# An attention and gated MLP kernel: nine pieces of fill among each of the last three pairs' ends, their stores on ScalarE's queue, and the first pair's order k, q, rests

## The chip, the cores and the metric

The kernel runs on one core of one Trainium2 chip. A core has a matrix engine (TensorE, PE in the views; PEld is its weight load), VectorE (DVE), ScalarE (ACT), GpSimd (POOL), and SyncE (SP), which here only issues transfers. ScalarE issues transfers too, from its own queue. The metric is the time of one execution in microseconds on the device.

## The reference

A linear attention whose features are `exp(±(x @ w_phi - max|x @ w_phi|))`, and behind it an MLP with a gate, on 4608 tokens (8 batches of 576), 8 heads of 64, model width 512, inner width 1536.

```python
def phi(x):
    proj = np.einsum('bhsd,df->bhsf', x, w_phi)
    proj = proj - np.max(np.abs(proj), axis=-1, keepdims=True)
    return np.concatenate([np.exp(proj), np.exp(-proj)], axis=-1)
q_p, k_p = phi(q), phi(k)
kv = np.einsum('bhsf,bhsd->bhfd', k_p, v)
num = np.einsum('bhsf,bhfd->bhsd', q_p, kv)
x = num / (np.einsum('bhsf,bhf->bhs', q_p, k_p.sum(2))[..., None] + 1e-6)   # then to (tokens, 512)
xn = x / np.sqrt(np.mean(x * x, axis=-1, keepdims=True) + 1e-6) * rms_g
g = xn @ w_gate
out = (g / (1 + np.exp(-g)) * (xn @ w_val)) @ w_out
```

## The kernel before

Products are made to nearly float32's precision from operands that are split into a high and a low part (`_split`: a ScalarE copy to the high part, a VectorE subtraction for the low one) and three matmuls each. The instructions are written in Python order, and a scheduler that works with modelled times orders them on each engine. `late()` restrains it: what is written inside is issued only after the latest instruction so far of ScalarE, VectorE and GpSimd. A queue of transfers runs in its own order, and an issue that has to wait holds up what is behind it.

**Stage one, the attention.** The loop over `i` works on 32 pairs of heads (`PR = 32`; a batch has four pairs) as a pipeline of four parts, merged by `_merge` at chosen fractions of an iteration: `front(i)` transposes q, k and the rests (the last 64 tokens of q and k together, "r") and projects them; `mid(i-1)` takes the exponentials and sums `kv` into `acc`; `back(i-2)` computes numerators and denominators (`num`) and, in `inv`, sends the denominators through memory and back (`dd`, `dr`, a reciprocal on VectorE, `di`, `rc`) to spread their inverses; `last(i-3)` multiplies (`fin`) and stores to `xs`. The loop has three more iterations than pairs, in which the last pairs' ends run. Each iteration also decodes a piece of the MLP's weights.

**Fill.** When a batch is finished, two blocks of 288 columns of `xs` are ready for the first 3 of 12 column tiles of the MLP's two first products, without the norm, which is applied later. `load_x` fetches a block (two slots of x, on ScalarE's queue), `fill` splits it (`xo`) and gives six pieces (`unit`): 12 matmuls into `fp`, a ScalarE copy to `fo` (three buffers), and a store to `gvs`. There are 16 blocks and so 96 pieces. A quota issues some at the end of each iteration, as long as more than `RES = 30` pieces are left. What is left runs behind the loop, six at a time.

**Block 0 of stage two** is fetched at i = 27 (`x0`), into one of the two slots, so that `load_x` rests in iterations 27 and 28; `prep(0)`, its norm, is written after iteration 29.

**Stage two** runs the other 9 column tiles in 12 blocks of 384 columns (`gv`), `gv_raw` the 3 from the fill, and stage three the last product.

Of the kernel before, what the change touches and what calls it, by code (L numbers as in the profile page):

```python
# [58 lines left out]
def _split(nc, hi, lo, x, hi_copy=None, lo_eng=None):  # L59
    (hi_copy or nc.scalar.copy)(hi, x)  # L60
    (lo_eng or nc.vector).tensor_tensor(lo, x, hi.bitcast(F32), ALU.subtract)  # L61


def _merge(streams):


    todo = []
    for n, st in enumerate(streams):
        for i, piece in enumerate(st):
            at = (i + 0.5) / len(st)  # L70
            if isinstance(piece, tuple):
                at, piece = piece
            todo.append((at, n, i, piece))
    for _, _, _, piece in sorted(todo, key=lambda t: t[:3]):
        piece()


def _spread(pieces, a, b):
    return [(a + (b - a) * (n + 0.5) / len(pieces), p) for n, p in enumerate(pieces)]
# [3 lines left out]
def kernel(ctx: ExitStack, tc: tile.TileContext, q, k, v, w_phi,  # L83
                         w_gate, w_val, w_out, rms_g, out):
    nc = tc.nc
# [4 lines left out]
    N = B * S  # L90
# [6 lines left out]
    J1 = 3  # L97
    T = 384
    NB = N // T
    TF = S // 2  # L100
# [26 lines left out]
    gvv = gvs.rearrange("(j w p) n -> j p w n", w=2, p=128)  # L127
# [12 lines left out]
    def fetch(bk, n=T, queue=None):  # L140
        x = xips[-1 if bk % 2 else 0].tile([128, NC * T], F32, name="x")[:, 0:NC * n].rearrange("p (c t) -> p c t", c=NC)
        (queue or nc.sync).dma_start(out=x, in_=xsv[:, :, bk * n:(bk + 1) * n])
        return x
# [23 lines left out]
    ps_f = ctx.enter_context(tc.tile_pool(name="ps_f", bufs=2, space=PSUM))  # L167
# [3 lines left out]
    waiting = set()  # L171

    @contextmanager
    def late():

        ins = nc.cur_bb.bb.instructions
        n = len(ins)
        with ExitStack() as es:
            for eng in LATE:
                for i in reversed(ins[-300:]):  # L180
                    if i.engine == eng and i.name not in waiting:
                        es.enter_context(tc.issue_after(i))
                        break
            yield
        waiting.update(i.name for i in nc.cur_bb.bb.instructions[n:])
# [27 lines left out]

    vms = [const.tile([128, 2, T0, D + 1], F32, name=f"vm{i}") for i in range(3)]
    vrs = [const.tile([128, 2, D + 1], F32, name=f"vr{i}") for i in range(3)]
    for vm, vr in zip(vms, vrs):
        nc.gpsimd.memset(vm, 1.0)
        nc.gpsimd.memset(vr, 1.0)
        nc.gpsimd.memset(vr[64:128, 0], 0.0)
        nc.gpsimd.memset(vr[0:64, 1], 0.0)  # L220
# [31 lines left out]
    def decode_pieces(jobs, dec):  # L252
        raws = {}

        def piece(i):
            if i == 0:
                raws[0] = _fetch(nc, dec, *jobs[0][:2])
            raw = raws.pop(i)
            if i + 1 < len(jobs):
                raws[i + 1] = _fetch(nc, dec, *jobs[i + 1][:2])  # L260
            with late():
                jobs[i][2](_decode(nc, dec, raw, jobs[i][1]))
        return [lambda i=i: piece(i) for i in range(len(jobs))]
# [22 lines left out]
    def front(pr):  # L286
        d = st[pr]
        f = {n: d[n].rearrange("p h t d -> p (h t d)") for n in ("kt", "qt")}
        us = {n: [f[n + "t"][:, i * 128:(i + 1) * 128] for i in range(4)] for n in "kq"}
        us["r"] = [d["rb"].rearrange("p a d -> p (a d)")]  # L290
        d["y"] = {}
        hl = {}

        def trans(n):
            m = len(us[n]) * 128
            tp = ps_s.tile([128, 512], F32, name="sm")
            for j, u in enumerate(us[n]):
                nc.tensor.transpose(out=tp[:, j * 128:(j + 1) * 128], in_=u, identity=ident)
            th = wk.tile([128, 512], F32R, name="th")
            tl = wk.tile([128, 512], F32R, name="tl")  # L300
            _split(nc, th[:, 0:m], tl[:, 0:m], tp[:, 0:m])
            hl[n] = (th, tl)

        def proj(n, u0):
            th, tl = hl[n]
            m = min(2, len(us[n]) - u0)
            pp = ps_p.tile([128, 4, F], F32, name="pp")
            for j in range(m):
                o = pp[:, 2 * j:2 * j + 2].rearrange("p a f -> p (a f)")
                cs = slice((u0 + j) * 128, (u0 + j + 1) * 128)  # L310
                nc.tensor.matmul(o, th[:, cs], wh, start=True, stop=False)  # L311
                nc.tensor.matmul(o, th[:, cs], wl, start=False, stop=False)
                nc.tensor.matmul(o, tl[:, cs], wh, start=False, stop=True)  # L313
            mx = wk.tile([128, 4], F32, name="mx")
            nc.vector.tensor_reduce(mx[:, 0:2 * m], pp[:, 0:2 * m], axis=AX.X, op=ALU.max,  # L315
                                    apply_absolute_value=True)
            y = wk.tile([128, 4 if n != "r" else 2, F], F32, name="y" + n, bufs=3 if n != "r" else 2)
            nc.vector.tensor_tensor(y[:, 0:2 * m], pp[:, 0:2 * m],  # L318
                                    mx[:, 0:2 * m].unsqueeze(2).broadcast_to([128, 2 * m, F]), ALU.subtract)
            d["y"][n, u0 // 2] = y  # L320

        return [lambda: trans("r" if pr else "k"), lambda: trans("k" if pr else "r"),
                lambda: proj("r", 0), lambda: proj("k", 0), lambda: trans("q"), lambda: proj("k", 2), lambda: proj("q", 0), lambda: proj("q", 2)]

# [132 lines left out]
    fills = []  # L457
    blocks = list(range(N // TF))

    def fill(bk, x):  # L460
        xhl = xfp.tile([128, 2, NC, TF], F32R, name="xo")
        xx = dict(h=xhl[:, 0], l=xhl[:, 1])
        with late():
            for c in range(0, NC, 2):
                _split(nc, *(a[:, c:c + 2] for a in (xx["h"], xx["l"], x)))

        def unit(j, wi):
            js = slice(j * 128, (j + 1) * 128)
            fp = ps_f.tile([128, T], F32, name="fp")
            i = 0  # L470
            for c in range(NC):
                a, al = wf1[wi][0][:, c, js], wf1[wi][1][:, c, js]
                for w, x in ((a, "h"), (a, "l"), (al, "h")):
                    nc.tensor.matmul(fp[:, 0:TF], w, xx[x][:, c], start=(i == 0), stop=(i == 3 * NC - 1))  # L474
                    i += 1
            o = xm.tile([128, T], F32, name="fo", bufs=3)[:, 0:TF]
            nc.scalar.copy(o, fp[:, 0:TF])  # L477
            nc.sync.dma_start(out=gvv[j][:, wi, bk * TF:(bk + 1) * TF], in_=o)
        return [lambda j=j, wi=wi: unit(j, wi) for j in range(J1) for wi in range(2)]

    PR = B * NP
    early, decs_late = decode_jobs()
    decs = decode_pieces(early, dec)
    RES = 5 * J1 * 2
    units, here = [], []
    dq = quota = 0.0

    def load_x():
        while fills and len(here) < 2:
            bk = fills.pop(0)  # L490
            here.append((bk, fetch(bk, TF, nc.scalar)))

    def landed():
        if here:
            units.extend(fill(*here.pop(0)))

    load(0)
    nc.sync.dma_start(out=g, in_=rms_g.rearrange("(c p) -> p c", p=128))
    load(1)
    for i in range(PR + 3):  # L500
        streams = []
        if i < PR:
            streams.append(_spread(front(i), -0.2, 0.7))
        if 0 <= i - 1 < PR:
            streams.append(_spread(mid(i - 1), -0.2, 1.1))
        if 0 <= i - 2 < PR:
            streams.append(back(i - 2))
        if 0 <= i - 3 < PR:
            streams.append(last(i - 3))
        dq += 1  # L510
        dl, decs = decs[:int(dq)], decs[int(dq):]
        dq -= int(dq)
        streams.append(dl)
        _merge(streams)

        if i == PR - 3:
            with late():
                nxt = prep(0, x0, ps_f, "fp")
        if len(units) <= 3:
            landed()  # L520
        if len(units) + (len(fills) + len(here)) * J1 * 2 > RES:
            quota += (N // TF * J1 * 2 - RES) / (PR - 4)
            nf = int(quota)
            quota -= nf
            now, units[:] = units[:nf], units[nf:]
            _merge([now])
        if i == PR - 5:
            x0 = fetch(0)
        if not PR - 5 <= i < PR - 3:
            load_x()  # L530
        if i + 2 < PR:
            load(i + 2)
    while units or here or fills:
        if len(units) <= 6:
            landed()
        now, units[:] = units[:6], units[6:]
        _merge([now])
        load_x()
    a_ctx.close()

# [86 lines left out]
    PRE = 4  # L627
    wos_ops = []
    load_gv(0)
    xb = {0: nxt}  # L630

    LAST = [*range(JL, JN), *range(JL)]
    for bk in range(NB):
# [172 lines left out]
```

## Time and profile before

| | us |
|---|---|
| median of 3 runs | 1333.65 (1332.86 to 1335.17) |
| the profiled execution | 1339.35 |
| its span in the trace | 1337.6 |

The engines' busy time over the whole span is in the page's first section. A row of the windows gives, for a stretch of time, the busy time of each engine and the clock that TensorE was granted (1.00 is full). A row of the timeline has its start, its length, engine, line, operation, what is written from what (buffer numbers left out) and, in brackets, how long the engine stood before it and what ended that. "x12" is a group of 12.

### The profile page before, as it was taken

What the parts mean: (1) busy time and instruction counts of PE and PEld (TensorE: products, weight loads), DVE (VectorE), ACT (ScalarE), POOL (GpSimd) and SP (SyncE); (2) the same over time, 40 slices, a digit from 0 to 9 for tenths busy, and PEclk for the clock granted to TensorE, in tenths of its full rate; (3) what the DMA queues carried; (4) which work ended last, traced back from release to release, by engine and by line L of the source; (5) the groups of instructions that cost most, each with busy time, mean ns of one, the idle gap of its engine ahead of it and who ended that gap; (6) DMA issues with size and microseconds to landing.
All of it is one profiled execution on the core that took longest, in us unless ns stands there. A gap on an engine that the chain in (4) does not pass through costs nothing.

```text
span 1337.6 us, 25479 instructions
## 1 busy us (share of the span) xinstructions
PE 1288.5 (96%) x9396; PEld 1275.6 (95%) x9396; DVE 885.0 (66%) x1301; ACT 711.0 (53%) x1510; POOL 605.5 (45%) x568
## 2 busy tenths in 40 slices
PE   7989999999999896899999999999999999999998
PEld 7989899999999896899999999999999999999998
DVE  7899788778778773313456656655534498777784
ACT  5988877778778782434344344443333334434332
POOL 3766565555555570000233223233221078788684
PEclk9999999999999898999999999999999999999999
DMA  5555556566555434843454454554433534554451
GB/s 159 127 147 156 161 158 165 167 170 169 157 164 161 123 95 127 249 153 126 141 170 140 157 168 133 166 168 140 133 115 108 183 111 126 150 166 127 142 168 54
DMA packets 204524, 197.22 MB, mean 147 GB/s; under 512 B 69552, under 2 KB 186416, under 8 KB 204400
## 3 DMA queue, kind: packets, MB, share of 16 engines
q1 hardware_dynamic: 186448, 181.44, 45.2%
q10 hardware_dynamic: 17952, 14.16, 3.8%
q8 instruction: 74, 1.21, 0.4%
q14 instruction: 50, 0.41, 0.1%
HBM read 126.04 MB, written 69.50 MB: 146 GB/s over the span
## 4 chain that ended last, share of the span: by engine, by line
PE 57%; DMA 3%; DVE 1%; ACT 0%; issue 0%; POOL 0%; ACTq 0%; SPq 0%; DVEq 0%
PE fp L588 17%; PE gp L588 16%; PE gd L742 6%; PE gz L742 6%; PE gy L742 5%; PE fp L474 4%; PE fp L742 3%; DMA wc<-wvs 1%; DMA gvs<-fo 1%; DMA rc<-di 0%; PE sm L415 0%; DMA dd<-nd 0%; ACT fo L477 0%; POOL s2l L61 0%; DVE a12l L61 0%
## 5 line engine op out<-in xcount | busy, mean ns | idle before, releaser
L380 POOL TENSOR_TENSOR ql<-eq,qh 128x256 fp32r<-128x256 f32 x256 | 217.7, 882 | 67.3 <-issue 39.5
L588 PE MATMUL gp<-xb,wv 128*128 128x384 f32 x864 | 161.9, 334 | 0.8 <-ACT wv L60 0.8
L588 PE MATMUL fp<-xb,wg 128*128 128x384 f32 x864 | 161.0, 334 | 0.0
L573 DVE TENSOR_TENSOR h<-sl,gp 128x384 f32<-128x384 f32 x108 | 59.6, 552 | 144.2 <-PE gp L588 75.6
L588 PEld LDWEIGHTS gp<-xb,wv 128*128 128x128 f32 x864 | 150.7, 188 | 1.0 <-ACT wv L60 1.0
L571 ACT ACTIVATE sl<-fp 128x384 f32<-128x384 f32 x108 | 52.8, 489 | 185.6 <-PE fp L588 170.7
L588 PEld LDWEIGHTS fp<-xb,wg 128*128 128x128 f32 x864 | 150.7, 188 | 0.0
L54 POOL TENSOR_TENSOR wa<-raw,wa 128x192 f32<-128x192 f32 (+1 forms) x112 | 66.2, 613 | 162.2 <-issue 58.6
L351 PE MATMUL acc<-vm,ek 128*128 128x65 f32 x1024 | 131.8, 271 | 0.0
L315 DVE TENSOR_REDUCE mx<-pp 128x4 f32<-128x512 f32 (+1 forms) x160 | 100.6, 632 | 43.0 <-PE pp L313 41.5
L351 PEld LDWEIGHTS acc<-vm,ek 128*128 128x128 f32 x1024 | 128.1, 195 | 0.4 <-ACT ek L338 0.4
L151 POOL TENSOR_TENSOR ss<-ss,sq 128x384 f32<-128x384 f32 x36 | 37.6, 1044 | 160.6 <-ACT sq L150 160.6
L61 POOL TENSOR_TENSOR xb<-x,xb 128x1536 fp32r<-128x1536 f32 x12 | 42.5, 3540 | 132.3 <-ACT xb L60 124.6
L474 PE MATMUL fp<-xo,fg 128*128 128x288 f32 x576 | 92.8, 302 | 5.7 <-ACT fo L477 3.4
L376 ACT ACTIVATE qh<-sm 128x512 fp32r<-128x512 f32 (+1 forms) x192 | 97.3, 507 | 0.0
L474 PE MATMUL fp<-xo,fv 128*128 128x288 f32 x576 | 92.2, 300 | 4.4 <-ACT fo L477 4.4
L311 PE MATMUL pp<-wh,th 128*128 128x256 f32 x288 | 89.0, 310 | 2.7 <-DVE yr L318 2.1
L474 PEld LDWEIGHTS fp<-xo,fg 128*128 128x128 f32 x576 | 81.7, 190 | 7.4 <-ACT fo L477 4.4
L474 PEld LDWEIGHTS fp<-xo,fv 128*128 128x128 f32 x576 | 81.7, 190 | 5.1 <-ACT fo L477 5.1
L61 POOL TENSOR_TENSOR s2l<-st,s2h 128x768 fp32r<-128x768 f32 x18 | 43.5, 2419 | 95.0 <-ACT s2h L60 47.6
L375 ACT ACTIVATE eq<-sm 128x512 f32<-128x512 f32 x128 | 78.4, 612 | 14.1 <-PE sm L364 13.2
L313 PE MATMUL pp<-wh,tl 128*128 128x256 f32 x288 | 83.0, 298 | 1.8 <-DVE tl L61 1.8
(198 smaller groups left out, 3801.8 us busy)
## 6 DMA issues: line engine op xcount, KB each, us to landing
hs<-h SPq DMA_DIRECT2D x144, 192.0 KB
ht<-hs SPq DMA_DIRECT2D x18, 1536.0 KB
gvs<-fo SPq DMA_DIRECT2D x96, 144.0 KB
gvr<-gvs SPq DMA_DIRECT2D x36, 384.0 KB
rc<-di SPq DMA_DIRECT2D x32, 288.0 KB
x<-xs ACTq DMA_DIRECT2D x16, 576.0 KB
x<-xs SPq DMA_DIRECT2D x12, 768.0 KB
kt<-in_k_dram SPq DMA_DIRECT2D x32, 256.0 KB
```

What stands on the lines that cost most here:

```text
L54: nc.gpsimd.tensor_tensor(a[:, h], lf[:, h], a[:, h], ALU.mult)
L61: (lo_eng or nc.vector).tensor_tensor(lo, x, hi.bitcast(F32), ALU.subtract)
L311: nc.tensor.matmul(o, th[:, cs], wh, start=True, stop=False)
L313: nc.tensor.matmul(o, tl[:, cs], wh, start=False, stop=True)
L315: nc.vector.tensor_reduce(mx[:, 0:2 * m], pp[:, 0:2 * m], axis=AX.X, op=ALU.max, apply_absolute_value=True)
L351: nc.tensor.matmul(acc[:, sg, h], e[h][:, sg, j], vm[:, h, j], start=False, stop=(h == 1 and j == T0 - 1))
L375: nc.scalar.activation(ei[:, sg], yi, AF.Exp, scale=1.0 - 2.0 * sg)
L376: nc.scalar.activation(hi[:, sg], yi, AF.Exp, scale=1.0 - 2.0 * sg)
L380: nc.gpsimd.tensor_tensor(lo[:, sg, cs], ei[:, sg, cs], hi[:, sg, cs].bitcast(F32), ALU.subtract)
L474: nc.tensor.matmul(fp[:, 0:TF], w, xx[x][:, c], start=(i == 0), stop=(i == 3 * NC - 1))
L588: nc.tensor.matmul(gp[:, 0:T], w, e[:, c], start=(i == 0), stop=(i == 3 * NC - 1))
L742: nc.tensor.matmul(place[n], a[:, kp], w[:, o], start=(first and kp == 0 and i == 0), stop=(kp == KP - 1 and i == 2), skip_group_check=True)
```

## The change

```diff
@@ late()
-                    if i.engine == eng and i.name not in waiting:
+                    if i.engine == eng and i.name not in waiting and not isinstance(i, mybir.InstDMACopy):
@@ the constant tiles
-    for vm, vr in zip(vms, vrs):
+    for vm in vms:
         nc.gpsimd.memset(vm, 1.0)
+    for vr in vrs:
         nc.gpsimd.memset(vr, 1.0)
@@ front(pr)
+        if pr == 0:
+            return [lambda: trans("k"), lambda: proj("k", 0), lambda: trans("q"), lambda: proj("k", 2),
+                    lambda: trans("r"), lambda: proj("r", 0), lambda: proj("q", 0), lambda: proj("q", 2)]
@@ fill(bk, x)
-        def unit(j, wi):
+        def unit(j, wi, queue):
...
-            nc.sync.dma_start(out=gvv[j][:, wi, bk * TF:(bk + 1) * TF], in_=o)
-        return [lambda j=j, wi=wi: unit(j, wi) for j in range(J1) for wi in range(2)]
+            queue.dma_start(out=gvv[j][:, wi, bk * TF:(bk + 1) * TF], in_=o)
+        return [lambda q=None, j=j, wi=wi: unit(j, wi, q or nc.sync) for j in range(J1) for wi in range(2)]
...
+    END = 9
+    nxt = []
@@ load_x() and landed()
-            here.append((bk, fetch(bk, TF, nc.scalar)))
+            here.append((bk, fetch(0, T, nc.scalar) if bk is None else fetch(bk, TF, nc.scalar)))
...
-        if here:
+        if here and here[0][0] is None:
+            with late():
+                nxt.append(prep(0, here.pop(0)[1], ps_f, "fp"))
+        elif here:
             units.extend(fill(*here.pop(0)))
+
+    def more():
+        if len(units) <= 3:
+            landed()
+            load_x()
+        if units:
+            units.pop(0)(nc.scalar)
@@ the loop over i
+        if i >= PR:
+            streams.append([more] * END)
         _merge(streams)
-        if i == PR - 3:
-            with late():
-                nxt = prep(0, x0, ps_f, "fp")
...
+        if i < PR:
...
-        if i == PR - 5:
-            x0 = fetch(0)
-        if not PR - 5 <= i < PR - 3:
-            load_x()
+        if i == PR + 1:
+            fills.append(None)
+        load_x()
...
     while units or here or fills:
...
-        _merge([now])
+        _merge([[lambda u=u: u(nc.scalar) for u in now]])
```

The quota issues pieces only while `i < PR`. In the three iterations behind, nine calls of `more` are merged among the ends of the last pairs; each issues one piece, and splits and fetches a block when three or fewer are left. Their stores, and those of all pieces behind the loop, go to ScalarE's queue; the quota's stay on SP's. Block 0's fetch and norm go through the list of fills (the entry `None`), put there at i = 33, ahead of the last batch's two blocks. x is fetched in iterations 27 and 28 too. `late()` does not take a transfer for an engine's latest instruction any more. In the first pair the rests come behind k and q.

Of the fill's 1152 matmuls, 408 stood ahead of the last pair's transposes of q, 114 from there to the last numerators, and 630 behind; now it is 504, 72 and 576.

The first place is on ScalarE, at the end of the third last pair's k exponentials. There `wa` and `raw` are the decoding of a weight, `ss` and `sq` the squares of block 0's norm, `eqr` and `qh` the exponentials of the rests of q. Before:

```order
L48 ACTIVATE wa<-raw 128x384
L49 ACTIVATE raw<-raw 128x384
L147 ACTIVATE ss<-x 128x384
L150 ACTIVATE sq<-x 128x384
L375 ACTIVATE eqr<-sm 128x128
L376 ACTIVATE qh<-sm 128x2x64
```

Now:

```order
L48 ACTIVATE wa<-raw 128x384
L49 ACTIVATE raw<-raw 128x384
L379 ACTIVATE eqr<-sm 128x128
L380 ACTIVATE qh<-sm 128x2x64
L379 ACTIVATE eqr<-sm 128x128
```

The squares left this place; the norm now stands on ScalarE behind the attention, among the copies of fill.

The second place is on VectorE at the end of the attention. `yq` is the last pair's projection of q, `nd` the multiplication in `fin`, `dr` the reciprocal in `inv`, `kv1l` the low part of the last pair's `kv`, and `xo` the split of a block of fill. Before:

```order
L318 TENSOR_TENSOR yq<-pp,mx 128x512
L442 TENSOR_TENSOR nd<-nd,rc 64x576
L443 TENSOR_TENSOR nd<-nd,rc 64x576
L425 RECIPROCAL dr<-dr 128x9
L55 TENSOR_TENSOR wa<-wp,wa 128x384
L442 TENSOR_TENSOR nd<-nd,rc 64x576
L443 TENSOR_TENSOR nd<-nd,rc 64x576
L425 RECIPROCAL dr<-dr 128x9
L61 TENSOR_TENSOR kv1l<-acc,kv1h 128x4x65
L61 TENSOR_TENSOR xo<-x,xo 128x576 x2
```

Now:

```order
L319 TENSOR_TENSOR yq<-pp,mx 128x512 x2
L446 TENSOR_TENSOR nd<-nd,rc 64x576
L447 TENSOR_TENSOR nd<-nd,rc 64x576
L429 RECIPROCAL dr<-dr 128x9
L55 TENSOR_TENSOR wa<-wp,wa 128x384
L61 TENSOR_TENSOR kv1l<-acc,kv1h 128x4x65
L61 TENSOR_TENSOR xo<-x,xo 128x576 x2
L446 TENSOR_TENSOR nd<-nd,rc 64x576
L447 TENSOR_TENSOR nd<-nd,rc 64x576
L61 TENSOR_TENSOR xo<-x,xo 128x576 x2
L429 RECIPROCAL dr<-dr 128x9
```

One pair's `nd` and the next one's `dr` moved from ahead of `kv1l` to behind it.

The third place is where the last pair's result is stored (`xs`), on SP's queue, with the transfers of its denominators and the fill's stores (`gvs`). Before:

```order
L419 DMA dd<-nd 1x576
L478 DMA gvs<-fo 128x288
L423 DMA dr<-dd 128x9
L478 DMA gvs<-fo 128x288
L426 DMA di<-dr 128x9
L478 DMA gvs<-fo 128x288
L428 DMA rc<-di 64x1152
L478 DMA gvs<-fo 128x288 x2
L448 DMA xs<-nd 128x64
L449 DMA xs<-nd 128x512
L478 DMA gvs<-fo 128x288 x31
```

Now, on SP's queue:

```order
L423 DMA dd<-nd 1x576
L453 DMA xs<-nd 128x512
L427 DMA dr<-dd 128x9
L430 DMA di<-dr 128x9
L432 DMA rc<-di 64x1152
L452 DMA xs<-nd 128x64
L453 DMA xs<-nd 128x512
```

And on ScalarE, from there on (`wc` is a tile of stage two's weights, cast to `wg` and `wv`):

```order
L481 COPY fo<-fp 128x288
L579 DMA wc<-wgs 128x4x128
L482 DMA gvs<-fo 128x288
L579 DMA wc<-wvs 128x4x128
L142 DMA x<-xs 128x4x288
L481 COPY fo<-fp 128x288
L60 CAST wg_0_8791<-wc 128x512
L579 DMA wc<-wgs 128x4x128
L482 DMA gvs<-fo 128x288
```

The stores left SP's queue there and stand on ScalarE's, between its copies, the x loads and the weight loads.

More of the change, by code (lines that the diff above doesn't have):

```diff
@@ L513 @@
         streams.append(dl)
+        if i >= PR:
+            streams.append([more] * END)
         _merge(streams)
-        if i == PR - 3:
-            with late():
-                nxt = prep(0, x0, ps_f, "fp")
[L519 to L525, printed above, removed]
-            _merge([now])
-        if i == PR - 5:
-            x0 = fetch(0)
-        if not PR - 5 <= i < PR - 3:
-            load_x()
+        if i < PR:
+            if len(units) <= 3:
+                landed()
+            if len(units) + (len(fills) + len(here)) * J1 * 2 > RES:
+                quota += (N // TF * J1 * 2 - RES) / (PR - 4)
+                nf = int(quota)
+                quota -= nf
+                now, units[:] = units[:nf], units[nf:]
+                _merge([now])
+        if i == PR + 1:
+            fills.append(None)
+        load_x()
         if i + 2 < PR:
@@ L536 @@
         now, units[:] = units[:6], units[6:]
-        _merge([now])
+        _merge([[lambda u=u: u(nc.scalar) for u in now]])
         load_x()
@@ L629 @@
     load_gv(0)
-    xb = {0: nxt}
+    xb = {0: nxt[0]}
     LAST = [*range(JL, JN), *range(JL)]
```

## The prediction

> **What bounds the kernel now.** I read the page's first section, then busy time by stretch, then single stretches in order of time.
>
> ```profile
> span 1337.6 us, 25479 instructions
> PE 1288.5 (96%) x9396; PEld 1275.6 (95%) x9396; DVE 885.0 (66%) x1301; ACT 711.0 (53%) x1510; POOL 605.5 (45%) x568
> ```
>
> TensorE is busy 1288.5 of 1337.6 us. The change takes no matmul away, so it can gain only from TensorE's 49 idle us, and from time in which TensorE runs at half its clock. The windows show where that is (columns: stretch, its length, busy time of PE, PEld, DVE, ACT, POOL, then the granted clock, DMA share, GB/s).
>
> ```profile
> core 0: us, PE busy (x) PEld busy (x) DVE busy (x) ACT busy (x) POOL busy (x), PEclk, DMA share, GB/s
> 60.00:100.00 40.00, 35.50 (x289) 34.03 (x289) 37.91 (x69) 34.53 (x87) 26.48 (x34) 1.00 0.56 150
> 100.00:425.00 325.00, 319.15 (x2629) 314.49 (x2628) 263.59 (x458) 253.46 (x632) 187.05 (x229) 1.00 0.59 164
> 425.00:620.00 195.00, 174.49 (x1260) 170.62 (x1259) 87.17 (x135) 106.48 (x246) 53.33 (x61) 0.95 0.49 145
> 620.00:1337.60 717.60, 709.86 (x4846) 708.86 (x4844) 449.27 (x547) 272.92 (x445) 306.19 (x190) 1.00 0.44 141
> ...
> 515.00:530.00 15.00, 12.84 (x83) 12.40 (x82) 3.12 (x5) 4.78 (x10) 0.00 (x0) 0.89 0.61 163
> 530.00:545.00 15.00, 10.36 (x72) 9.65 (x71) 6.29 (x10) 5.62 (x12) 0.00 (x0) 1.00 0.73 215
> 545.00:570.00 25.00, 22.35 (x155) 21.56 (x154) 7.62 (x12) 9.72 (x21) 0.00 (x0) 1.00 0.77 232
> ...
> 570.00:620.00 50.00, 48.62 (x360) 47.92 (x359) 9.18 (x13) 21.30 (x49) 3.04 (x3) 1.00 0.41 137
> ...
> 449.70:460.20 10.50, 10.47 (x49) 10.48 (x50) 4.31 (x8) 5.15 (x12) 6.38 (x8) 0.51 0.38 113
> 507.80:511.20 3.40, 3.38 (x14) 3.38 (x15) 1.30 (x2) 0.99 (x2) 0.00 (x0) 0.50 0.08 22
> 525.00:528.40 3.40, 3.40 (x16) 3.40 (x16) 0.00 (x0) 1.38 (x3) 0.00 (x0) 0.50 0.76 165
> ```
>
> From 620 us on TensorE idles 1% and decides alone: what is won earlier arrives at the end whole. From 100 to 425 it idles 1.8%. From 425 to 620, the last pairs and the fill behind them, it idles 20.5 us, and in three stretches of 10.5, 3.4 and 3.4 us it is busy at half clock, which loses 5.2 + 1.7 + 1.7 = 8.6 us. So 29 us can be had there, and no more. That is where nearly all of the diff lies.
>
> **Part 1: block 0's norm leaves the attention stage.** Before, the norm of the second stage's first block (`prep(0)`) is written after iteration 29; now it comes out of the same list as the fill, behind the attention.
>
> ```profile
> 448.07 0.52 ACT L147 ACTIVATE ss<-x 128x384 f32<-128x384 f32 x1 [2.38 <-DMA x<-xs]
> 449.73 0.57 PE L298 MATMUL sm<-ident,kt 128*128 128x128 f32 x2 [2.30 <-ACT qh L376]
> ```
>
> ScalarE reaches the norm's first square before its x has landed and stands 2.38 us; the exponentials behind it in its queue come late, TensorE idles 2.30 us, and the 10.5 us at half clock follow. The order shows the squares gone from that place. It also shows fill there: the last four pairs had 12, 0, 0 and 12 matmuls of fill between their q transposes and now have 19, 29, 42 and 30, since the x slot that was kept free for block 0 is not kept free any more. Gain 2.3 + 5.2 = **7.5 us**. The norm itself now stands behind 372 fill matmuls, 31 units. A unit is 12 matmuls and takes 1.60 us (the next starts at 572.73):
>
> ```profile
> 571.13 1.76 PE L474 MATMUL fp<-xo,fv 128*128 128x288 f32 x12
> ...
> 492.14 3.49 POOL L61 TENSOR_TENSOR xb<-x,xb 128x1536 fp32r<-128x1536 f32 x1
> ```
>
> 31 units are 50 us of cover for work that is off TensorE. One thing is not covered: the last block's x load now waits in ScalarE's queue until GpSimd has finished the norm's 3.49 us split, with copies of fill queued behind. That costs between 0 and 3.5 us; TensorE has four units and 36 matmuls of stage two in hand there, so I take **1**.
>
> **Part 2: the last pair's numerators.**
>
> ```profile
> 502.53 0.75 DVE L442 TENSOR_TENSOR nd<-nd,rc 64x576 f32<-64x576 f32 x1 [6.49 <-DMA rc<-di]
> 507.27 0.22 DVE L425 RECIPROCAL dr<-dr 128x9 f32<-128x9 f32 x1 [3.21 <-DMA dr<-dd]
> 507.40 0.37 DVE L61 TENSOR_TENSOR kv1l<-acc,kv1h 128x260 fp32r<-128x260 f32 x1
> ...
> 507.82 0.61 PE L415 MATMUL sm<-qh,kv1l 128*128 128x288 f32 x1 [5.88 <-DVE kv1l L61]
> ```
>
> VectorE's `kv1l`, which the last numerators need, stands behind the end of one pair (waiting for a DMA, 6.49 us) and the reciprocal of the next (3.21 us). In the new order both, and the multiply between them, come after it. TensorE's 5.88 us and the 1.7 us at half clock behind them go: **7.6 us**. What comes late next: the last pair now has no fill between its projections and its numerators, where it had 8 units (13 us). TensorE is then at the pace of VectorE. Such pairs are in the row of 60 to 100 us, three of them, and leave 40 - 35.5 = 4.5 us of TensorE idle, 1.5 each. Then the next fill needs the next block's split, which now follows `kv1l`:
>
> ```profile
> 522.20 1.25 ACT L60 CAST xo<-x 128x576 fp32r<-128x576 f32 x2
> ...
> 523.36 1.43 DVE L61 TENSOR_TENSOR xo<-x,xo 128x576 fp32r<-128x576 f32 x2 [0.25 <-issue]
> ```
>
> The two overlap by half a pass, so 2 us or a little more, against 14 matmuls in hand (1.9 us at 1.60/12 each) less the start of the split: 1 us. Charge **2.5**, with 0 and 5.9 (all the old wait) as its ends. If that wait halves the clock for the shortest stretch seen, 3.4 us, it costs **1.7** more; the longest seen, 10.5 us, costs 5.2. I take the short one, as the idle is spread over the pair.
>
> The page "TensorE: Matmul & The Clock Gate" of the Trainium skill (section "Why this matters for your kernels") asks only that gaps stay under about 3 us; by it the 1.7 us would not be charged and the sum would be 2 us better. The trace differs, a gap of 2.30 us having been enough, so I keep the charge.
>
> **Part 3: the fill's stores move from SP's queue to ScalarE's.** This holds for the pieces among the ends and for all behind them.
>
> ```profile
> 525.96 1.01 SPq L478 DMA_DIRECT2D gvs<-fo  x2
> 533.33 0.32 SPq L448 DMA_DIRECT2D xs<-nd  x1
> ...
> 534.18 34.42 SPq L478 DMA_DIRECT2D gvs<-fo  x17
> ...
> 521.90 0.40 ACT L477 COPY fo<-fp 128x288 f32<-128x288 f32 x1 [2.18 <-DMA gvs<-fo]
> ...
> 532.02 0.40 ACT L477 COPY fo<-fp 128x288 f32<-128x288 f32 x1 [3.36 <-DMA gvs<-fo]
> ...
> 522.92 0.40 PE L474 MATMUL fp<-xo,fg 128*128 128x288 f32 x1 [1.30 <-ACT xo L60]
> 524.17 1.17 PE L474 MATMUL fp<-xo,fg 128*128 128x288 f32 x6 [0.85 <-DVE xo L61]
> ...
> 532.47 1.86 PE L474 MATMUL fp<-xo,fv 128*128 128x288 f32 x12 [1.85 <-ACT fo L477]
> 536.35 0.93 PE L474 MATMUL fp<-xo,fg 128*128 128x288 f32 x5 [2.02 <-ACT fo L477]
> ```
>
> SP's queue is in order. From 526 to 533 it stands before the store of the last pair's result, and the store of the copy made at 528.26 goes out after it. Three `fo` buffers fill up, ScalarE's copies wait 2.18 and 3.36 us, the splits behind the first come late, and TensorE idles 1.30 + 0.85 + 1.85 + 2.02 = 6.0 us and then 3.4 us at half clock (1.7). With the stores on ScalarE, behind nothing but ScalarE's own work, I take **7.7 us** as gone. The rest, 9.45 idle from 515 to 570 less 6.0, and 1.4 from 570 to 620, I leave as it is.
>
> Against it stands what the stores meet on the new queue:
>
> ```profile
> 524.82 0.37 ACTq L142 DMA_DIRECT2D x<-xs  x1
> ...
> 561.22 6.07 DMA gvs<-fo
> ...
> 592.60 4.38 DMA gvs<-fo
> ```
>
> An issue there takes 0.37 us. Copy (0.40) and issue make 0.77 us of a 1.60 us unit, so the issues fit. But stores now queue with x loads and stage two's weight loads, and while the weights came in (DMA 77% busy from 545 to 570) one landing held the chain 6.07 us, later one 4.38. With three buffers a unit cannot go faster than (0.77 + landing)/3, which passes 1.60 us at a landing of 4.0. For 16 units beside the weight loads I take 4.4 and so 0.12 us each, **2 us**; bounds 0 and, at 6.07, 11. As the wait for a landing is on the issuing side in both orders, half a microsecond for its lateness is added: charge **2.5**.
>
> **Part 4: the first pair's order** k, q, then projections, then the rests; GpSimd's memsets of `vr` go behind those of `vm`.
>
> ```profile
> 5.31 0.41 ACT L60 CAST wh<-wa 128x256 fp32r<-128x256 f32 x1
> ...
> 7.41 0.45 PE L298 MATMUL sm<-ident,rb 128*128 128x128 f32 x1 [2.62 <-DMA rb<-in_q_dram]
> ...
> 8.37 0.56 PE L311 MATMUL pp<-wh,th 128*128 128x256 f32 x1
> ...
> 10.67 0.42 DVE L315 TENSOR_REDUCE mx<-pp 128x2 f32<-128x256 f32 x1 [2.19 <-PE pp L313]
> ```
>
> TensorE waits 2.62 us for the rests' DMA with q behind it, and the projections start at 8.37. Now `wh` (from 5.31 at the latest, 0.41) and one cast of k of about that length stand ahead of them, so they can start at about 6.2, and VectorE, which decides from 60 to 100 us (37.9 of 40 busy), gets its first reduction some 2.2 us earlier. The identity comes behind one more `vm` memset in place of a smaller one. I take **2 us**; bounds 2.2 and, if that memset costs as much as the cast, -0.4. The `late()` edit only leaves DMA issues out as anchors: 0, as ScalarE's queue has few of them before the end; a changed order from 100 to 425 us can move the 5.9 idle us there by some 3 either way.
>
> **Sum.** 7.5 + 7.6 + 7.7 + 2 = 24.8 gained; 1 + 2.5 + 1.7 + 2.5 = 7.7 charged: **17 us**. The profiled execution took 1339.35 us around its span of 1337.6, 5.7 above the shown median of 1333.65; 17 off either gives 1322 under the profiler and **1317** as a median.
>
> **Rivals.** *The queue buys nothing*: the landings, not SP's order, hold the copies. Part 3 falls out with its charge (7.7 - 2.5 = 5.2): 1322. For it: landings of 4 to 6 us on a busy memory. Against: the 526 to 533 hole in SP's queue is a wait for VectorE. The page "DMA: Bandwidth & Descriptors" of the Trainium skill, section "Issuing engines are not separate DMA queues", is on this side: all queues run on the same engines, so another issuer saves only its issue time; the seven-microsecond hole in SP's rows is more than that, so here the trace differs. *The clock stays down*: the last pair without fill idles 4 us and runs 10.5 us at half clock, 1.5 + 3.5 more: 1322. For it: that was the sequel of 2.30 us. Both together: 1327. *All is covered*: no charge arises: 1309.
>
> *Slower*: stores on ScalarE's queue land behind x and weights in the same queue, all 54 units from the last numerators on. It decides from a landing of 4.0 us. Without the 2.5 charge the gain is 19.5, or 0.36 us per unit, and (0.77 + landing)/3 = 1.96 at a landing of 5.1: from there on the kernel is slower than before. At 6.07 for all, each unit takes 2.28, and 54 x 0.68 = 37 us are lost: 1351. Against it: from 570 to 620 us, with 41% DMA, TensorE idled 1.4 us of 50.
>
> **How the numbers follow.** Forecast 1317 (1311 to 1323 alone): 0.50. Queue buys nothing 0.14; clock stays down 0.12; both 0.05; all covered 0.08; slow landings 0.11, of which a third near 5.0 us, about as before, and two thirds above. Leaving out that last case and the far tails, the range is 1307 to 1329. A measurement tells 0.2% (2.7 us) from no change: faster 0.89, the same 0.04, slower 0.07.
>
> **What would show it.** Part 1: no half clock around the third last pair, and no ScalarE wait for x there. Part 2: `kv1l` right behind `kv1h`, and a wait of 1 to 3 us, not 5.9, before the last numerators. Part 3: no copy of fill that waits for a store while SP stands, but some that wait while weights load. Part 4: the first reduction near 8.4 us. TensorE's idle and half-clock loss over the 195 us should fall from 29 to about 14. It is wrong if copies wait for stores all through the fill behind the attention.

## The result, and the profile after

| | before | after |
|---|---|---|
| median, us | 1333.68 (1332.86 to 1335.17, 4 runs) | 1350.50 (1348.99 to 1352.95, 4 runs) |
| the profiled execution, its span, us | 1339.35, 1337.6 | 1351.39, 1349.6 |
| ratio | 1 | 1.0114 (95%: 1.0088 to 1.0141) |

The kernel became 1.1% slower, where 1.2% faster was forecast. The windows say where. In both fences a row is a stretch of the span, its length, the busy time of PE, PEld, DVE, ACT and POOL, then the granted clock. TensorE's idle time is the length less PE. The clock is averaged over the whole row, idle time too, so the loss at half clock is taken from the stretches at half clock themselves: half of the time in which TensorE is busy in them. Before:

```profile
0.00:100.00 100.00, 85.05 (x668) 81.59 (x669) 84.95 (x163) 78.10 (x191) 58.95 (x89) 1.00 0.55 145
100.00:200.00 100.00, 96.13 (x783) 92.48 (x782) 85.76 (x155) 81.21 (x202) 62.06 (x77) 1.00 0.58 157
425.00:505.00 80.00, 73.14 (x556) 71.91 (x554) 58.14 (x92) 62.68 (x150) 50.30 (x58) 0.93 0.39 108
505.00:640.00 135.00, 121.35 (x820) 118.71 (x821) 38.93 (x57) 52.72 (x109) 4.04 (x4) 0.96 0.54 167
```

After:

```profile
0.00:100.00 100.00, 88.68 (x686) 84.90 (x687) 87.12 (x163) 78.11 (x192) 59.39 (x89) 1.00 0.54 142
100.00:200.00 100.00, 88.89 (x677) 86.35 (x676) 80.92 (x140) 72.99 (x183) 56.60 (x69) 0.91 0.57 148
425.00:505.00 80.00, 78.24 (x632) 77.53 (x631) 61.53 (x104) 59.16 (x148) 44.83 (x55) 0.98 0.44 128
505.00:640.00 135.00, 115.04 (x757) 110.29 (x756) 35.72 (x51) 55.66 (x119) 15.35 (x14) 0.92 0.51 156
```

Idle and half-clock loss, in us, before to after: 15.0 + 0 to 11.3 + 0; 3.9 + 0 to 11.1 + 7.6; 6.9 + 5.1 to 1.8 + 1.7; 13.7 + 3.5 to 20.0 + 7.0. So the start gains 3.6, where 2 were forecast, and the end of the attention gains 8.5. But 14.8 are lost from 100 to 200 us, where next to no cost was expected, and 9.9 in the fill behind the attention. The sum is 12.6, and 200 to 425 us gained 1.3; the spans differ by 12.0. What is left at the end of the attention is, in the main, one wait of TensorE with 3.4 us at half clock behind it:

```profile
501.32 0.49 PE L419 MATMUL sm<-ql,kv0h 128*128 128x288 f32 x1 [1.49 <-POOL ql L384]
```

**The early loss.** The timelines of TensorE, ScalarE and VectorE of the kernel after, at the end of a pair's `acc`:

```profile
110.66 0.40 PE L419 MATMUL fp<-qh,kv0h 128*128 128x288 f32 x1 [2.77 <-ACT kv0h L60]
114.36 0.61 PE L419 MATMUL fp<-qh,kv0l 128*128 128x288 f32 x1 [1.90 <-DVE kv0l L61]
```

```profile
101.75 0.51 ACT L60 CAST fv<-wa 128x384 fp32r<-128x384 f32 x1 [1.07 <-DVE wa L236]
103.54 0.95 ACTq L142 DMA_DIRECT2D x<-xs  x2
104.53 0.28 ACT L379 ACTIVATE eqr<-sm 128x128 f32<-128x128 f32 x1 [2.27 <-PE fp L419]
...
110.19 0.41 ACT L60 CAST kv0h<-acc 128x260 fp32r<-128x260 f32 x1
```

```profile
111.58 1.17 DVE L447 TENSOR_TENSOR nd<-nd,rc 64x576 f32<-64x576 f32 x1
113.81 0.22 DVE L429 RECIPROCAL dr<-dr 128x9 f32<-128x9 f32 x1 [1.05 <-DMA dr<-dd]
113.94 0.37 DVE L61 TENSOR_TENSOR kv0l<-acc,kv0h 128x260 fp32r<-128x260 f32 x1
```

TensorE waits for `kv0h`, then for `kv0l`, and runs at half clock from 112.4 to 126.0 us. ScalarE, in front of `kv0h`, stands 2.27 us, and the row blames a matmul. But between the cast and the exponential stand two issues of x's fetch: the engine stands until `xs` has landed, and everything behind is late. VectorE has `kv0l` behind a product and a reciprocal that waits for its transfer. That is the pattern that Part 2 of the prediction removed from the last pair; here the new order made it. Before, the fetches (at 100.64 and 101.15) didn't hold ScalarE, `kv0l` stood ahead of those instructions, and the two waits were under 1 us.

**The late loss.** TensorE's waits in the fill, and the norm's first and last steps on ScalarE and GpSimd:

```profile
558.20 3.25 PE L478 MATMUL fp<-xo,fv 128*128 128x288 f32 x12 [4.02 <-ACT fo L481]
584.11 0.69 PE L156 MATMUL fp<-sq,ones 128*128 128x384 f32 x1 [6.95 <-ACT sq L60]
596.51 0.79 PE L603 MATMUL gp<-xb,wv 128*128 128x384 f32 x3 [0.77 <-ACT xb L60]
600.02 4.26 PE L603 MATMUL gp<-xb,wv 128*128 128x384 f32 x14 [2.72 <-POOL xb L61]
```

```profile
557.22 0.62 ACT L60 CAST wg<-wc 128x512 fp32r<-128x512 f32 x1 [3.81 <-DMA wc<-wgs]
...
578.25 0.53 ACT L147 ACTIVATE ss<-x 128x384 f32<-128x384 f32 x1
...
583.54 0.51 ACT L60 CAST sq<-ss 128x384 fp32r<-128x384 f32 x1 [1.10 <-POOL ss L151]
```

```profile
596.53 3.43 POOL L61 TENSOR_TENSOR xb<-x,xb 128x1536 fp32r<-128x1536 f32 x1 [11.40 <-ACT xb L60]
```

From its first square (578.25) to the end of the last split (599.96) block 0's norm takes 21.7 us: squares and sums that go back and forth between ScalarE and GpSimd, a matmul, a root, products, the split. TensorE stands for it at the norm's matmul and at stage two's first products, 6.95 + 0.77 + 2.72 = 10.4 us, and loses 4.7 us at half clock from 580 to 604 us. The 4.02 us are a copy behind a cast whose weights were late; 2.4 us at half clock go with them.

### The profile page after: what moved, and what is told of

Read it like the earlier page. It is cut to its first block, busy times and chain, and to the rows that moved or that the text cites. A ratio compares the mean times of both kernels' runs of the same rounds, so it can differ in the third digit from the quotient of the medians.

```text
span 1349.6 us, 25422 instructions
## 1 busy us (share of the span) xinstructions
PE 1296.9 (96%) x9396; PEld 1282.8 (95%) x9396; DVE 886.1 (66%) x1301; ACT 709.1 (53%) x1509; POOL 607.1 (45%) x568
## 4 chain that ended last, share of the span: by engine, by line
PE 82%; DMA 5%; DVE 5%; ACT 4%; POOL 1%; issue 1%; ACTq 0%; SPq 0%; DVEq 0%; POOLq 0%
PE fp L603 17%; PE gp L603 16%; PE fp L478 8%; PE acc L355 7%; PE gd L757 5%; PE gz L757 5%; PE gy L757 5%; PE sm L419 4%; PE fp L419 3%; PE fp L757 2%; PE pp L314 2%; PE pp L312 2%; PE sm L368 2%; PE pp L313 2%; PE sm L299 2%; DMA gvs<-fo 1%
## 5 line engine op out<-in xcount | busy, mean ns | idle before, releaser
L384 POOL TENSOR_TENSOR ql<-eq,qh 128x256 fp32r<-128x256 f32 x256 | 221.2, 896 | 93.8 <-issue 46.6
L478 PE MATMUL fp<-xo,fv 128*128 128x288 f32 x576 | 97.7, 308 | 5.3 <-ACT fo L481 5.3
```

The costliest lines, as they stand in the source:

```text
L384: nc.gpsimd.tensor_tensor(lo[:, sg, cs], ei[:, sg, cs], hi[:, sg, cs].bitcast(F32), ALU.subtract)
```

## The experiments

Two theories: **A**, the opening (first pair's order and memsets) costs the early loss; **B**, the late loss comes from the stores' queue (B1) or from the norm's new place (B2). Times are compared by the ratio to runs of the kernel before on the same chip (their median moved between 1332.8 and 1336.5).

**The opening alone**, on the kernel before: `front`'s new order for `pr == 0` and the memsets, nothing else.

> The kernel before with the opening alone (first pair in the order k, q, rests; memsets reordered). Theory A (the new opening is what costs the changed kernel some 15 us between 100 and 180 us, after a gain of 3.7 in the first 100): 1342 to 1347, with a half clock that starts near 112 us. Rival (the early loss comes from another part of the change, or from the two together): 1329 to 1332, the gain of 3.7 us alone, with full clock from 100 to 180.

1345.13 us, 1.0079 (1.0052 to 1.0106). Theory A holds. The waits are there (2.90 and 1.59 us), and the windows from 0 to 200 us are those of the changed kernel:

```profile
0.00:100.00 100.00, 88.87 (x684) 85.26 (x685) 86.33 (x162) 77.94 (x192) 59.57 (x89) 1.00 0.54 141
100.00:200.00 100.00, 89.56 (x666) 87.02 (x665) 79.16 (x139) 72.67 (x181) 56.78 (x69) 0.90 0.56 145
```

**The change without the opening**: both of those edits undone.

> The changed kernel with the old opening; all else as changed. Theory A: the loss of 15 us between 100 and 180 us goes and the gain of 3.7 before it too: 1338 to 1341, with the tail's waits between 540 and 625 us as in the changed kernel. Rival (the opening isn't the cause): 1352 to 1355 with the half clock near 112 us still there.

1334.38 us, 1.0009 (0.9994 to 1.0025): 1% better than with it, and 4 us better than expected.

**The stores back on SP's queue**, in the changed kernel: `units.pop(0)(nc.sync)` in `more`, and `u(nc.sync)` behind the loop.

> The changed kernel with the stores of the last pieces of fill back on SyncE's queue. Theory B1 (stores on ScalarE's queue beside the weight loads cost the tail): the 3.81 and 4.02 us waits near 557 and the half clock behind them go, some 10 us: 1339 to 1343. Rival (the queue costs nothing, or SyncE's own waits cost as much): 1347 to 1353, with waits for stores at other places between 540 and 600 us.

1349.13 us, 1.0096 (1.0058 to 1.0133). B1's 1339 to 1343 us fail: the wait of 4.02 us is gone (the longest for a copy is 2.7), but the time isn't measurably better (the intervals overlap widely and leave room for some microseconds); 18.6 us of idle stay from 505 to 640 us against 20.0, with the norm's 6.2 and 2.7 us among them.

**The norm at its old place**, in the changed kernel:

```diff
-        if i == PR + 1:
-            fills.append(None)
-        load_x()
+        if i == PR - 3:
+            with late():
+                nxt.append(prep(0, x0, ps_f, "fp"))
+        if i == PR - 5:
+            x0 = fetch(0)
+        if not PR - 5 <= i < PR - 3:
+            load_x()
```

> The changed kernel with the norm of the first block of stage two back among the third last pair; nine pieces of fill in each of the last pairs and the stores on ScalarE's queue stay. Theory B2 (the norm behind the fill costs its own waits there, 6.95 + 2.72 us of idle and some 6 us of half clock, while its old place costs 7.5 us): 1340 to 1346, waits for the cast of the squares gone from 584 us, an idle stretch and a half clock back near 470 us. Rival (the old place costs as much as the new one): 1349 to 1353.

1336.29 us, 1.0028 (1.0009 to 1.0048): better than expected, so B2 is the larger part of the late loss. The expected half clock near 470 us didn't come back in its profile, where the first square waits 0.39 us for its x; that profile is of a run of 1332.69 us, below the median.

**Both undone**: old opening and old norm; nine pieces in each end with stores on ScalarE, and `late()`, are what is left of the change. Beside it the same with stores on SP.

> The changed kernel with the old opening and with the norm at its old place: what is left of the change are the nine pieces of fill in each of the last pairs and their stores on ScalarE's queue. If the opening and the moved norm are the two parts that cost (theory), this is the kernel with the norm at its old place (1336.29) less the 5 us of net loss that the opening leaves in the first 200 us of that run: 1324 to 1331, faster than before. Rival (the parts act only together, or the pieces of fill gain nothing by themselves): 1332 to 1337.

> The same with the stores on SyncE's queue: nine pieces in each of the last pairs are all that is left of the change. If the queue of the stores is worth as little as in the changed kernel (1349.13 against 1350.5): within 2 us of the run beside it. Rival (the queue of the stores does gain when the norm is out of its way, up to the 7.7 us of store waits before): 4 to 8 us slower than the run beside it.

1325.19 us, 0.9937 (0.9916 to 0.9957), and 1328.90 us, 0.9960 (0.9940 to 0.9979). So the pieces are worth some 0.4 to 0.6%, and what was undone costs. How much of it is the queue isn't settled: the two intervals overlap. What the norm's move does is read from the rows of 425 to 640 us, first with the old opening and the new place (1334.38), then with the old place (1325.19):

```profile
425.00:505.00 80.00, 78.80 (x637) 78.13 (x636) 54.94 (x90) 60.79 (x152) 42.95 (x53) 1.00 0.43 129
505.00:640.00 135.00, 117.05 (x759) 112.81 (x758) 42.35 (x59) 54.70 (x108) 14.95 (x10) 0.95 0.50 155
```

```profile
425.00:505.00 80.00, 74.36 (x584) 72.72 (x584) 61.06 (x94) 63.75 (x152) 51.52 (x58) 0.98 0.41 120
505.00:640.00 135.00, 127.65 (x865) 124.82 (x864) 40.94 (x60) 56.37 (x115) 10.41 (x8) 1.00 0.56 173
```

The new place gains 5.6 + 1.6 - 1.2 = 6.0 us inside the attention and costs (18.0 + 4.6) - 7.4 = 15.2 us behind it. But little of the 6.0 is the hold that Part 1 of the prediction names. TensorE's two longest waits in that row, with the old place:

```profile
449.27 1.10 PE L351 MATMUL acc<-vm,ek 128*128 128x65 f32 x8 [1.43 <-ACT ek L338]
501.47 0.61 PE L415 MATMUL sm<-qh,kv1l 128*128 128x288 f32 x1 [2.64 <-DVE kv1l L61]
```

Behind the norm's first square TensorE waits 1.43 us, and full clock follows. The 2.64 us and the 1.6 us at half clock behind them are the last pair's `kv1l`: with the norm at its old place it stands again on VectorE behind the products of `fin`, which stand 7.75 us for a transfer. It is so in five of the six kernels that have the nine pieces and the old place (2.6 to 3.5 us), and in none with the new place.

**What gives the opening's gain back?** Three kernels take one hold after the other out of the opening alone. First the first two blocks' fetch goes to SP (`nc.sync if bk < 2 else nc.scalar`), which leaves TensorE's and VectorE's order as it was:

> The kernel before with the new opening alone (1345.13), and the fetches of the first two blocks of x on SyncE's queue instead of ScalarE's; TensorE's and VectorE's order are the same in both. Theory (the opening brings ScalarE 3 us earlier to the fetch of x, where it stands 2.4 us until xs has landed; behind it the cast of kv0h, TensorE's wait of 2.90 us, then half clock): that wait falls below 1 us, no half clock between 100 and 140 us, 1330 to 1336. Rival (the work of VectorE and ScalarE bounds the stretch, and TensorE, 3.7 us ahead, has to wait there whatever holds them): waits of 4 us and the half clock stay, 1341 to 1347.

1340.54 us, 1.0040 (1.0023 to 1.0056): a part, neither theory alone.

```profile
109.02 0.40 PE L419 MATMUL fp<-qh,kv0h 128*128 128x288 f32 x1 [1.23 <-ACT kv0h L60]
113.00 0.61 PE L419 MATMUL fp<-qh,kv0l 128*128 128x288 f32 x1 [2.17 <-DVE kv0l L61]
```

The first wait fell from 2.90 to 1.23 us, so ScalarE did stand for the fetch; the second grew. Next, for two pairs, `fin` (1.15 in place of 0.65) and `inv` (1.12 in place of 0.79) are written later, so that `kv0l` stands ahead of them:

> The kernel with the new opening and x fetched on SyncE (1340.54), and for two pairs the reciprocal and the products of fin are written later, so that on VectorE the low cast kv0l at 113 us stands ahead of them instead of behind. Theory (two holds cost the opening its gain: ScalarE's fetch of x, already taken away, and kv0l behind the products and a reciprocal that waits for its transfer): the wait of 2.17 us goes too, no half clock between 100 and 140 us, 1328 to 1335. Rival (the stretch is bound by the work of VectorE and ScalarE, the wait turns up at the next matmul): 1338 to 1344 with the half clock.

1337.24 us, 1.0008 (0.9989 to 1.0027), no longer slower than before. The wait for `kv0l` went, and the next one rose. TensorE, and VectorE ahead of it:

```profile
118.46 0.58 PE L314 MATMUL pp<-wh,tl 128*128 128x256 f32 x1 [3.02 <-DVE tl L61]
```

```profile
112.50 0.21 DVE L429 RECIPROCAL dr<-dr 128x9 f32<-128x9 f32 x1 [2.89 <-DMA dr<-dd]
```

This looks like the rival, an engine at its limit. But VectorE isn't busy there, it stands for a transfer. So one pair's reciprocal was moved into the next iteration, behind the low parts:

> The kernel of the last step of the opening (1337.24), with one pair's reciprocal of the denominators in the next iteration: on VectorE it stands behind kv0l, the split of x and the next pair's low parts, instead of ahead of them with its wait for the transfer (2.89 us). Theory (holds in the in-order queues give the opening's gain back): TensorE's wait of 3.02 us at 118 falls below 1 us, TensorE idles under 6 us from 100 to 200 us with full clock, 1328 to 1333. Rival (VectorE's work bounds the stretch): TensorE waits as long at the next place, 7 to 9 us idle from 100 to 200, 1334 to 1340.

1333.58 us, 0.9997 (0.9976 to 1.0017).

```profile
100.00:200.00 100.00, 95.95 (x792) 93.56 (x791) 89.08 (x160) 82.48 (x207) 62.28 (x80) 1.00 0.62 167
```

4.1 us idle at full clock, with 11.6 from 0 to 100: 15.7 to the 200th microsecond, where the kernel before has 18.8. Holds in in-order queues had given the gain back, not VectorE's work. The 3.1 us are 0.23%, at the edge of the interval, so the time can neither show nor exclude them; the edit also shifted the schedule behind (in this profile 425 to 505 us idle 3 us more than before).

**Which half of the opening?** The order alone (old memsets), and the memsets alone on the 1325.19 us kernel:

> The kernel before with the order k, q, rests alone, the memsets in their old order. Theory (the order moves the schedule and costs, the memsets bring the first transposes 2 us earlier): the loss between 100 and 200 us is there, 1340 to 1349. Rival (TensorE runs ahead of ScalarE only because the memsets let it start earlier): no half clock there, 1330 to 1336.

> The nine pieces with stores on ScalarE's queue alone (1325.19), and the memsets in the new order with the first pair in the old one; TensorE's order is the same throughout. Theory (the memsets bring the first transposes some 2 us earlier and do no harm without the new order of the pair): 1322 to 1325. Rival (what is gained at the start is waited off at 110 us, or costs half clock there): 1325 to 1333.

1345.25 us, 1.0095 (1.0062 to 1.0127): the order is the costly half. 1330.27 us, 0.9960 (0.9943 to 0.9977): beside the old order the memsets gain nothing; with them TensorE is as idle in the first 100 us as without (15.0 and 14.9). The time lies in the rival's range, but the rival's wait isn't there (0.47 us at 110 us, full clock). Beside the new order they do gain: 11.1 us idle with both, 12.9 with the order alone.

**Why does the norm cost behind the attention?** In the change without the opening the norm is written in two steps: squares and sums, then its matmul and the rest behind the next six pieces.

> The changed kernel with the old opening (1334.38), and the norm behind the fill in two steps: the squares and sums first, its matmul only behind the next six pieces of fill, 60 matmuls (8 us) later in TensorE's order. Theory (the norm's new place costs because its matmul stands in TensorE's queue ahead of fill that could run, and waits 6.55 us for squares and sums that go back and forth between ScalarE and GpSimd; half clock follows): the wait falls below 1 us and the half clock behind it goes, 1323 to 1329. Rival (the norm is simply late, and the wait moves to stage two's first products, which then wait 7 us more for xb): 1332 to 1337.

1336.94 us, 1.0011 (0.9992 to 1.0029). The theory fails and the rival holds, to the microsecond:

```profile
572.69 0.44 PE L162 MATMUL fp<-sq,ones 128*128 128x384 f32 x1 [0.90 <-ACT sq L60]
581.20 1.33 PE L610 MATMUL gp<-xb,wv 128*128 128x384 f32 x3 [7.00 <-ACT xb L60]
584.71 7.69 PE L610 MATMUL gp<-xb,wv 128*128 128x384 f32 x29 [2.18 <-POOL xb L61]
```

The wait moved along the norm's chain. In TensorE's order 60 matmuls of fill (8 us) stand between the norm's matmul and stage two's first products in the changed kernel, here none, and 300 (40 us) in the 1325.19 us kernel, where the norm is at its old place. To tell this distance from the place in time, the same with block 0 put on the list at i = 28:

> The changed kernel with the old opening and the norm in two steps (1336.94), block 0 put on the list at i = 28: the norm's matmul stands behind 864 matmuls of fill instead of 1008, and stage two's first products right behind it, with 288 matmuls of fill after them. Theory (what counts is the fill between the norm's matmul and stage two's first products in TensorE's order, here none): TensorE still waits some 7 us for xb there, 1332 to 1339. Rival (the norm is too late in time, 144 matmuls or 19 us earlier is enough): the waits for xb fall below 2 us, 1324 to 1329.

1338.87 us, 1.0042 (1.0023 to 1.0061); the time and TensorE's row are as the theory expected:

```profile
563.02 1.33 PE L610 MATMUL gp<-xb,wv 128*128 128x384 f32 x3 [7.00 <-ACT xb L60]
```

18 us earlier, with 288 matmuls of fill still to come, TensorE waits the same 7.00 us. So in these kernels it is what stands between the norm and its first use that hides it, not what stands ahead of it.

**The edit of `late()`** undone in the 1325.19 us kernel, and **both causes repaired** in the change:

> The nine pieces with stores on ScalarE's queue (1325.19), with late() as it was before, so that an issue of a transfer may again be the instruction waited for. If the edit of late() is worth nothing: within 2 us of 1325.19. Rival (the edit carries part of the gain, because with stores on ScalarE the latest instruction there is often an issue that waits): 1328 to 1335.

> The change with both costs taken out: nine pieces with stores on ScalarE's queue and the norm at its old place (1325.19), and the new opening with its three holds removed (the first two fetches of x on SyncE, fin and the reciprocal of two pairs later). If the causes are independent: the 3.3 us that the opening keeps at 200 us come on top, 1319 to 1324. Rival (the shifted schedule costs elsewhere, as between 425 and 505 us in the run before, what the start gains): 1325 to 1331.

1329.01 us, 0.9977 (0.9957 to 0.9996): the interval just meets the other's, so the edit may be worth up to 0.4% or nothing. And 1324.13 us, 0.9938 (0.9916 to 0.9960): it beats both kernels, but not the one with the old opening (0.9937). The gain of the repaired opening, in the profile at 200 us, is too small for these intervals.

## Why the prediction was wrong

- **What bounds the kernel.** "29 us can be had there" was right, but the argument looked only at what could be won in that stretch. It took the 200 us ahead of it as given.
- **Part 1** failed in its charge. The charge of 1 us was some 15: 10.4 of waits and 4.7 at half clock in the changed kernel, 15.2 in the pair of kernels that differ in the norm's place. The failing sentence is "31 units are 50 us of cover": those units stand ahead of the norm. A chain that starts when ScalarE reaches it is hidden by what stands between it and its use, and the order had 60 matmuls (8 us) there for a chain of 21.7 us. The 3.49 us split was the only link that I charged. The gain of 7.5 was in the profile before, but it isn't a fixed price: in the twelve profiles with the norm at its old place TensorE's wait there goes from under 0.6 to 3.2 us, and half clock follows in four. In the pair above it was 1.4 us; that its row shows 6.0 in all, near 7.5, is luck.
- **Part 2** was right for the changed kernel: `kv1l` isn't waited for any more, and what came in its place, a wait of 1.49 us for `ql` with 3.4 us at half clock behind it, is of the size of the charges (2.5 and 1.7). From 425 to 505 us 1.8 us idle and 1.7 us of half-clock loss are left in all. But the sum took this gain as independent of Part 1, and it is not: `kv1l` is waited for again where the norm is at its old place.
- **Part 3** was mis-sized and nearly beside the point. Changing the queue alone did nothing measurable in the changed kernel, and 0.23%, not clear of the noise, where the norm is out of the way (0.9937 against 0.9960); 5.2 us net were forecast. The order of SP's queue wasn't what held the copies in the main; with stores on ScalarE copies still waited for landings (2.24 and 2.71 us at 566 and 577 us).
- **Part 4** failed in "some 3 either way". The start gained 3.6 us, more than the 2 expected. But the first pair's order shifted the schedule of the next pairs, and two in-order queues then held `kv0h` and `kv0l`: 7.2 us of idle and 7.6 of half clock. In three pairs of kernels that differ in the opening (with or without the norm at its old place, or with all else as before) it cost 0.8 to 1.05%.
- **The slower rival** named 1351 us, but for another mechanism: landings on ScalarE's queue. Taking the stores away from that queue left the time at 1349, so the agreement is chance.

By ratios: pieces with stores -0.63%, then the norm 0.72 and the opening 1.05%, or the opening first, 0.91, and then the norm, 0.86. Either way the steps lead to the measured 1.14% by construction; what they show is that the norm and the opening each cost about the same whether the other is there or not.

## What to carry to other kernels

Before work is called covered, count in the bound engine's order what stands between it and its first use, and set that against the whole chain in series, not against its longest link. Before two gains are added, ask whether the order that gives the one is still there without the other's edit. An edit at the start of a schedule has to be followed through the engines' orders to where something stands behind an instruction that waits for a transfer; there, a few microseconds won can come back as a gap that halves the clock. And a wait named in a profile may hide the next one in the same queue: take the holds away one by one until none is left before calling an engine the bound.

## What the runs showed of the hardware

The half clock behind nearly the same gaps is not the same from run to run. Up to some 420 us the opening alone and the changed kernel with the norm at its old place run the same order. In the profile of the first the waits were 2.90 and 1.59 us (clock in the third column from the end):

```profile
115.00:120.00 5.00, 5.00 (x25) 5.00 (x24) 3.72 (x6) 2.19 (x5) 3.74 (x4) 0.50 0.45 136
120.00:125.00 5.00, 5.00 (x24) 5.00 (x24) 1.26 (x3) 0.99 (x3) 0.00 (x0) 0.50 0.26 79
125.00:130.00 5.00, 5.00 (x38) 5.00 (x37) 2.54 (x5) 3.30 (x10) 0.70 (x1) 0.83 0.25 68
```

and in that of the second, with 2.79 and 0.72 us:

```profile
115.00:120.00 5.00, 4.28 (x18) 3.97 (x19) 4.32 (x7) 4.91 (x11) 3.83 (x5) 0.50 0.73 152
120.00:125.00 5.00, 5.00 (x41) 5.00 (x40) 3.28 (x8) 1.47 (x3) 2.43 (x3) 0.89 0.45 136
```

With 110 to 115 us (0.80 and 0.92) that is 13.7 and 6.9 us at half clock. A wait of 3.02 us (the kernel with `fin` and `inv` later, at 118 us) was followed by only 3.4. The lengths are near multiples of 3.4 us, and in every profile the stretches start whole multiples of 3.41 us apart (in the kernel before at 449.9, 504.5 and 525.0 us, 16 and 6 of them). The page "TensorE: Matmul & The Clock Gate" of the Trainium skill, section "Part 1: The HAM clock gate (the "warmup" mystery)", has activity judged in free-running windows of about that length; the traces agree.

Cut into windows of 3.41 us on that grid, the 17 profiles show from 60 to 640 us what precedes half clock. A window at full clock in which TensorE idled 1.9 us or more was followed by one at half clock in 39 of 39 cases; with 1.63 to 1.9 us it was 9 of 13; with less, 1 of 2724. So it was the idle time in one window that told, not the length of a gap, and where the cuts fall differs from profile to profile. At the norm's old place the 2.30 us of the kernel before lie in one window, and 10.2 us at half clock follow; in the kernel with `late()` undone 2.29 us are cut into 1.47 and 0.82, and none follow. How long half clock lasts stays open: of 54 windows at half clock in which TensorE idled at most 0.05 us, 14 were followed by another.

So a gap of two or three microseconds costs a chance of several more rather than a fixed price, and the runs of one kernel spread: 1332.41 to 1342.30 us for the second kernel of this section, 1329.30 to 1340.16 us in 29 runs of the kernel before.
